# Re-listing the first steps of a linear-attention and feed-forward kernel in an order found by search

## The chip, the cores and the metric

The kernel runs on one core of one Trainium2 chip. The core has five engines with a queue of instructions each: PE (TensorE, the matmuls), DVE (VectorE), ACT (ScalarE), POOL (GpSimd) and SP (SyncE, which only starts transfers here). The time is the device time of one execution in microseconds (us). It is given as the median of several runs; a separate profiled execution gives the trace.

## The reference

Two layers follow each other. The first is a linear attention with a decaying state, for 4 batches, 8 heads, 768 tokens and a head dimension of 48:

```python
for t in range(S):
    cur = np.einsum('bhd,bhe->bhde', u[None] * kt, vt)
    y[:, :, t] = np.einsum('bhd,bhde->bhe', rt, state + cur)
    state = w[None, :, :, None] * state + np.einsum('bhd,bhe->bhde', kt, vt)
...
h = x @ w_in
g = np.maximum(0.01 * h, h)
return (g @ w_out)
```

The second takes y as x, 3072 tokens by 384, through w_in (384 by 2048), a leaky ReLU and w_out (2048 by 384). Inputs and outputs are float32.

## The kernel before

The 768 tokens of a batch are cut into 6 chunks of 128. One pair n of chunk and batch (24 in all, n = 4 x chunk + batch) is the unit of work. Within a chunk the recurrence becomes matmuls: r and k are scaled by tables of powers of w, turned so that the head dimension lies on partitions, multiplied to a 128 x 128 matrix per head (masked to the tokens that lie earlier, with the term of u on its diagonal), and this matrix times v plus turned r times the state gives y. The state of a batch goes from pair n to pair n + 4. y is copied to bfloat16 as a slice of xT, the input of the second layer, which runs on 128 tokens (pairs 0 to 3) or 256 tokens (from pair 4 on) at a time.

All work is a list of named steps, the string ORDER. `run` (it reads the names from left to right) calls one function for each, and each function appends instructions to the program. Two things follow from a step's place in the list. First, every engine plays its own instructions in the order in which they were appended; nothing passes on an engine. The class Sched finds the data each step reads and writes and adds semaphore waits between engines where one needs another's result. Second, the eight PSUM banks are handed out and given back in the order of the list (`take`, `give`), so a step that takes a bank waits until the step that gave it back has read it.

The names of the steps, with n the pair:

- `k0`, `r0`: loads of pair 0 in float32 (`load_first`, L234). `k0` is issued by ACT, `r0` by SP. `kn`, `rn`, `vn` for the other pairs: loads issued by POOL (`load_one`, L243). `wi0` to `wi3` and `wo0` to `wo3`: quarters of w_in and w_out, issued by POOL (L253, L257). `w8`, `w`, `u8`, `u`: small rows of w and u, issued by SP.
- `c0q@`, `c0k@`: casts of pair 0's r and k to bfloat16 on DVE (L440). `Cw`, `Wl`, `E`: w as columns on PE (L557), its logarithm wcol and the turned tables on ACT (L576, L356). `bc`, `lnw`, `qtab`, `ktab`: w spread to all partitions on PE (L337), its logarithm and the two tables on ACT (L344, L351). `Cu`, `C`: the columns of w times u on PE and their copy on DVE (L568, L583), after `wu8` (L361). `u16`, `U`, `utab`: the table of u.
- `one`, `ones`, `qk0`, `v0z`, `v0y`, `wlz`, `zr`: memsets on DVE. `trow`, `tcol`: indices on POOL (L275, L270). `tri`, `id`, `id8`, `exps`: mask, identities and exponents from them, on DVE. `table`: ACT's load of its function table. `F9`, `F6`, `F4`: that many matmuls of ones by ones into a bank, whose result nobody reads (L290).
- `Pnq`, `Pnk`: scaled r and k on DVE (L392). `Tnq`, `Tnk` and `tnq`, `tnk`: turning on PE (L455) and the copy out on ACT (L473, on DVE for pair 0 with its tables, L468). From pair 6 on `XnT`, a transposing transfer issued by SP, takes their place.
- `Xn`, `Dn`, `Qn` for n up to 3: the diagonal term, as a product on DVE (L407), matmuls on PE (L512) and scaled v on DVE (L414). From pair 4 on `qn` are the row sums on DVE (L421, L423, L425) and `Qn` the diagonal tile on POOL (L432).
- `An`, `Mna`, `Mnb`: the matrix on PE (L484) and its masking on DVE, in two halves (L493, from pair 4 L497). `Yn`, `yn`: y on PE (L646, L653) and its copy to xT on ACT (L667). `Kn`, `Sn`, `sn`: k by v on PE (L538, L529) and the new state on DVE. `W`: the decay table for the state on ACT (L591).
- `Gn.f`, `gn.f`: four blocks of x by w_in for one pair on PE (L692) and their leaky ReLU on ACT (L703). `Jm.f`, `jm.f`: two blocks for two pairs. `Hn`, `hn`: the product with w_out on PE (L716), its copy on ACT (L728) and the store by SP.

Around the change the order is thus the list itself. Two lines say which queue the first loads stand in:

```python
eng, queue = {"k": ("act", A), "r": ("sp", SP)}[which]
add(eng, lambda: queue.dma_start(dst, src), W=[(which, n)], dma=f"{which}{n}")
```

The functions that read the list:

Of the kernel before, what the change touches and what calls it, by code (L numbers as in the profile page):

```python
# [18 lines left out]
E = 64  # L19
# [6 lines left out]
TURNED, DIAG, CARRY, EXACT, RAW = 6, 4, 4, 1, 1  # L26
STRIPS = 8
ORDER = """
w8 qk0 k0 v0z one r0 trow ones v0y tcol wlz r1 id8 F9 wi1 u8 zr table Cw Wl id E w bc lnw c0q@ T0q c0k@ tri u exps k1
T0k u16 wu8 Cu t0q t0k qtab P1q F6 k3 v3 U A0 ktab T1q v0 t1q X0 C D0 P1k T1k t1k F4 M0b P3k M0a T3k K3 utab X1 A1 D1  # L30
Q0 Y0 t3k P0k r3 P3q M1a T3q r2 P2q y0 k2 K0 M1b v1 Q1 W G0.1 Y1 t3q X3 wi3 A3 y1 g0.1 S3 T2q D3 G1.1 g1.1 k5 t2q r5
r4 P2k T2k wi2 S0 v2 M3b t2k Q3 G0.3 g0.3 G1.3 k4 M3a Y3 P5k A2 y3 P4q T4q v4 wi0 T5k v5 wo3 t4q g1.3 G3.1 q5 t5k Q5
G3.3 g3.3 P5q r6 wo2 X2 g3.1 M2b D2 wo1 G3.2 Q2 G0.2 g0.2 T5q t5q K2 P4k T4k M2a t4k S2 G1.2 g3.2 q4 Q4 K1 S1 Y2 A5 A4
G1.0 y2 G2.1 M5a G0.0 G2.3 M4a M5b Y5 g0.0 y5 M4b Y4 y4 G2.2 g2.2 K4 J2.4 j2.4 k6 wo0 J2.1 J2.2 g1.0 g1.2 S4 k7 P6q q6
j2.1 P6k P7k G2.0 r7 q7 X6T J2.6 j2.6 J2.3 j2.3 k8 G3.0 J2.7 j2.7 k9 r9 j2.2 J2.5 P7q g3.0 g2.3 X7T J2.0 H1 h1 r8 q8
g2.0 Q6 P9k j2.0 P8k H0 j2.5 H3 Q7 A6 P9q X9T P8q X8T v6 A7 M6a v7 M7a g2.1 H2 h2 v9 v11 v10 M6b Y6 M7b y6 Q8 q9 Y7 y7
K5 r11 K6 S6 r10 k10 S5 Q9 v8 K7 S7 h0 h3 k11 J3.0 j3.0 J3.1 j3.1 J3.2 j3.2 J3.3 j3.3 J3.4 j3.4 J3.5 j3.5 J3.6 j3.6
J3.7 j3.7 A8 A9 M8a M8b M9a M9b P10q P10k X10T P11q P11k X11T k12 r12 v12 k13 r13 v13 q10 Q10 q11 Q11 H4 h4 Y8 Y9 y8
y9 K8 K9 S8 S9 s8 s9 H5 h5 J4.0 j4.0 J4.1 j4.1 J4.2 j4.2 J4.3 j4.3 J4.4 j4.4 J4.5 j4.5 J4.6 j4.6 J4.7 j4.7 P12q P12k
X12T P13q P13k X13T q12 q13 A10 A11 M10a M10b M11a M11b k14 r14 v14 k15 r15 v15 Q12 Q13 H6 h6 H7 h7 Y10 Y11 y10 y11  # L40
K10 K11 A12 A13 M12a M12b M13a M13b S10 S11 P14q P14k X14T P15q P15k X15T s10 s11 q14 q15 J5.0 j5.0 J5.1 j5.1 k16 r16
v16 k17 r17 v17 Q14 Q15 J5.2 j5.2 J5.3 j5.3 J5.4 j5.4 J5.5 j5.5 J5.6 j5.6 J5.7 j5.7 H8 h8 H9 h9 Y12 Y13 y12 y13 K12
K13 A14 A15 M14a M14b M15a M15b S12 S13 P16q P16k X16T P17q P17k X17T s12 s13 q16 q17 J6.0 j6.0 J6.1 j6.1 k18 r18 v18
# [3 lines left out]
K17 A18 A19 M18a M18b M19a M19b S16 S17 P20q P20k X20T P21q P21k X21T s16 s17 q20 q21 J8.0 j8.0 J8.1 j8.1 k22 r22 v22  # L47
k23 r23 v23 Q20 Q21 J8.2 j8.2 J8.3 j8.3 J8.4 j8.4 J8.5 j8.5 J8.6 j8.6 J8.7 j8.7 H14 h14 H15 h15 Y18 Y19 y18 y19 K18
K19 A20 A21 M20a M20b M21a M21b S18 S19 P22q P22k X22T P23q P23k X23T s18 s19 q22 q23 J9.0 j9.0 J9.1 j9.1 Q22 Q23 J9.2
j9.2 J9.3 j9.3 J9.4 j9.4 J9.5 j9.5 J9.6 j9.6 J9.7 j9.7 H16 h16 H17 h17 Y20 Y21 y20 y21 A22 A23 M22a M22b M23a M23b  # L50
J10.0 j10.0 J10.1 j10.1 J10.2 j10.2 J10.3 j10.3 J10.4 j10.4 J10.5 j10.5 J10.6 j10.6 J10.7 j10.7 H18 h18 Y22 Y23 y22
y23 H19 h19 J11.0 j11.0 J11.1 j11.1 J11.2 j11.2 J11.3 j11.3 J11.4 j11.4 J11.5 j11.5 J11.6 j11.6 J11.7 j11.7 H20 h20
H21 h21 H22 h22
# [784 lines left out]
```

## Time and profile before

| what | value |
|---|---|
| median of 3 runs | 168.88 us (168.47 to 169.81) |
| profiled execution, its time | 167.93 us |
| profiled execution, its span (first to last instruction) | 166.1 us |
| busy share of PE, DVE, ACT, POOL | 96%, 65%, 54%, 66% |

The profile comes from one execution. Its page gives busy times by engine, the chain of work that ended last, and groups of instructions by line. Its timeline lists instructions in order of time: start, duration, engine, line, operation, output <- inputs, shapes, how many of a kind follow each other and, in brackets, how long the engine stood idle before and what ended that. "L392" is line 392 of the kernel. "PEld" is PE's loading of weights, "SPq", "ACTq" and "POOLq" an issue of a transfer on that engine's queue. A matmul's end is modelled, so a duration holds the way through the array too; the pitch from one start to the next is closer to what it costs.

### The profile page before, as it was taken

What the parts mean: (1) busy time and instruction counts of PE and PEld (TensorE: products, weight loads), DVE (VectorE), ACT (ScalarE), POOL (GpSimd) and SP (SyncE); (2) the same over time, 40 slices, a digit from 0 to 9 for tenths busy, and PEclk for the clock granted to TensorE, in tenths of its full rate; (3) what the DMA queues carried; (4) which work ended last, traced back from release to release, by engine and by line L of the source; (5) the groups of instructions that cost most, each with busy time, mean ns of one, the idle gap of its engine ahead of it and who ended that gap; (6) DMA issues with size and microseconds to landing.
All of it is one profiled execution on the core that took longest, in us unless ns stands there. A gap on an engine that the chain in (4) does not pass through costs nothing.

```text
span 166.1 us, 5157 instructions
## 1 busy us (share of the span) xinstructions
PE 158.9 (96%) x2220; PEld 120.6 (73%) x2220; DVE 107.8 (65%) x248; ACT 89.3 (54%) x168; POOL 110.4 (66%) x125
## 2 busy tenths in 40 slices
PE   2798999999999999999999999999999999999994
PEld 2576989985567668668768768768678668678663
DVE  7799998377688599958938939939939934000000
ACT  3856873865138438436536546447437438449121
POOL 8999798987999949999299299399380270000000
PEclk9999999999999999999999999999999999999999
DMA  7999999999999995999949949969960540011012
GB/s 107 145 141 162 170 188 193 178 150 165 99 153 233 119 167 128 125 159 151 146 105 116 145 112 110 113 160 103 137 148 14 99 126 4 0 47 51 37 57 97
DMA packets 101268, 20.19 MB, mean 122 GB/s; under 512 B 94459, under 2 KB 101246, under 8 KB 101246
## 3 DMA queue, kind: packets, MB, share of 16 engines
q0 software_dynamic: 76512, 10.03, 93.2%
q1 hardware_dynamic: 23694, 9.65, 27.9%
q8 instruction: 17, 0.28, 0.7%
q10 hardware_dynamic: 1040, 0.20, 0.6%
q14 instruction: 5, 0.04, 0.1%
HBM read 20.45 MB, written 4.72 MB: 152 GB/s over the span
## 4 chain that ended last, share of the span: by engine, by line
PE 85%; POOL 7%; DMA 4%; DVE 2%; issue 0%; ACT 0%; POOLq 0%
PE ps L716 38%; PE ps L692 36%; PE ps L653 6%; DMA r_sb<-in_r_dram 4%; PE ps L484 3%; POOL r_sb L243 2%; POOL k_sb L243 2%; POOL v_sb L243 2%; PE ps L529 1%; POOL w_in_sb L253 1%; DVE prod L407 1%; PE ps L538 1%; DVE s_tok L425 0%; PE ps L455 0%; POOL trow L275 0%
## 5 line engine op out<-in xcount | busy, mean ns | idle before, releaser
L692 PE MATMUL ps<-xT,w_in_sb 128*128 128x256 bf16 (+1 forms) x672 | 66.4, 257 | 0.2
L703 ACT ACTIVATE gT<-ps 128x512 bf16<-128x512 f32 x96 | 56.3, 598 | 16.1 <-PE ps L692 12.3
L716 PE MATMUL ps<-w_out_sb,gT 128*128 128x384 bf16 (+2 forms) x400 | 64.6, 320 | 0.0
L692 PEld LDWEIGHTS ps<-xT,w_in_sb 128*128 128x128 bf16 x672 | 57.0, 98 | 7.2 <-DVE sum_t L614 0.5
L432 POOL TENSOR_TENSOR at<-ident,s_tok 128x512 bf16<-128x512 bf16 x40 | 42.1, 1087 | 24.9 <-DVE s_tok L425 24.9
L716 PEld LDWEIGHTS ps<-w_out_sb,gT 128*128 128x128 bf16 x400 | 38.1, 98 | 23.1
L728 ACT ACTIVATE out_sb<-ps 128x384 f32<-128x384 f32 (+2 forms) x25 | 11.9, 479 | 51.1 <-PE ps L716 51.1
L497 DVE CAST_PREDICATED at<-mask,ps 128x512 bf16<-128x512 uint16 x40 | 24.9, 685 | 20.1 <-PE ps L484 19.9
L243 POOL DMA_DIRECT2D v_sb<-in_v_dram x24 | 22.1, 928 | 0.0
L243 POOL DMA_DIRECT2D k_sb<-in_k_dram x23 | 21.2, 927 | 0.0
L243 POOL DMA_DIRECT2D r_sb<-in_r_dram x23 | 21.1, 926 | 0.1
L423 DVE TENSOR_TENSOR rku<-r_sb,ku 128x384 bf16<-128x384 bf16 x20 | 12.2, 612 | 1.4 <-DMA r_sb<-in_r_dram 0.8
L667 ACT ACTIVATE xT<-ps 128x384 bf16<-128x384 f32 x24 | 10.8, 491 | 2.5 <-PE ps L653 2.4
L425 DVE TENSOR_REDUCE s_tok<-rku 128x8 f32<-128x384 bf16 x20 | 11.1, 553 | 0.7
L392 DVE TENSOR_TENSOR qk<-k_sb,ktab 128x384 bf16<-128x384 bf16 x23 | 10.0, 437 | 1.3 <-DMA k_sb<-in_k_dram 1.3
L653 PE MATMUL ps<-at,v_sb 128*32 128x128 bf16 x384 | 10.6, 219 | 0.0
L653 PEld LDWEIGHTS ps<-tp,st 128*32 128x32 bf16 x240 | 7.3, 96 | 3.0 <-issue 2.5
L392 DVE TENSOR_TENSOR qk<-r_sb,qtab 128x384 bf16<-128x384 bf16 x23 | 8.9, 390 | 0.4 <-DMA r_sb<-in_r_dram 0.2
L653 PE MATMUL ps<-tp,st 128*32 128x128 bf16 x240 | 9.1, 221 | 0.0
L653 PEld LDWEIGHTS ps<-at,v_sb 128*32 128x32 bf16 x384 | 8.6, 97 | 0.4
L605 DVE TENSOR_TENSOR sum_t<-ps,st 64x192 bf16<-64x192 f32 x24 | 8.5, 353 | 0.6
L421 DVE TENSOR_TENSOR ku<-k_sb,u_tab 128x384 bf16<-128x384 bf16 x20 | 7.9, 395 | 1.2 <-DMA k_sb<-in_k_dram 1.1
(67 smaller groups left out, 96.0 us busy)
## 6 DMA issues: line engine op xcount, KB each, us to landing
out_dram<-out_sb SPq DMA_DIRECT2D x23, 192.0 KB, 2.0
v_sb<-in_v_dram POOLq DMA_DIRECT2D x24, 96.0 KB, 4.5
r_sb<-in_r_dram POOLq DMA_DIRECT2D x23, 96.0 KB, 4.9
k_sb<-in_k_dram POOLq DMA_DIRECT2D x23, 96.0 KB, 4.7
w_in_sb<-in_moe_w_in_dram POOLq DMA_DIRECT2D x4, 384.0 KB, 6.6
w_out_sb<-in_moe_w_out_dram POOLq DMA_DIRECT2D x4, 384.0 KB, 7.2
tp<-qk SPq DMA_TRANSPOSE x18, 4.7
k_f<-in_k_dram ACTq DMA_DIRECT2D x1, 192.0 KB, 2.8
```

The costliest lines, as they stand in the source:

```text
L243: add("pool", lambda: G.dma_start(dst, src), R=pace, W=[(which, n)], dma=f"{which}{n}")
L392: add("dve", lambda: V.tensor_tensor(qk[iq][:, H * half:H * half + H, 0:D], hd(src), hd(tab[:, :]), ALU.mult), R=[(name, n), "qk"[half] + ...
L423: add("dve", lambda: V.tensor_tensor(rku[i2][:, :], r_of(n), ku[i2][:, :], ALU.mult), R=[("r", n), ("ku", i2)], W=[("rku", i2)])
L425: add("dve", lambda: V.tensor_reduce(s_tok[i2][:, :], hd(rku[i2][:, :]), AX.X, ALU.add), R=[("rku", i2)], W=[("s", i2)])
L432: add("pool", lambda hh=hh, s_of=s_of: G.tensor_tensor(at[ia][:, hh, :, :], ident[:, :].unsqueeze(1).to_broadcast([128, NP, 128]), s_of.un ...
L497: add("dve", lambda: V.copy_predicated(at[n % NAT][:, hh, :, :], mask[:, :].bitcast(mybir.dt.uint16).unsqueeze(1).to_broadcast([128, NP, 1 ...
L653: last = PE.matmul(ps_y[32 * q:32 * q + 32, 128 * s:128 * s + 128], a, m, start=not whole and step == 0, stop=step == len(columns[q]) - 1)
L667: add("act", lambda: A.activation(xT[ix][:, :, 128 * slot:128 * slot + 128], ps_y[:, 0:HD].rearrange("p (s t) -> p s t", t=128), AF.Copy), ...
L692: last = PE.matmul(ps_g[:, step * f:step * f + step], w_in_sb[:, s, 128 * fb:128 * fb + 128], xT[ix][:, s, t], start=s == 0, stop=s == NSL ...
L703: add("act", lambda: A.activation(gT[ig][:, fb0:fb0 + count, t], ps_g[:, :].rearrange("p (f t) -> p f t", t=128 * width), AF.Prelu, alpha= ...
L716: last = PE.matmul(ps_o[:, 0:c1 - c0], gT[ig][:, s, 128 * slot:128 * slot + 128], w_out_sb[:, s, c0:c1], start=s == 0, stop=s == NFB - 1)
L728: add("act", lambda: A.activation(out_sb[io][:, c0:c1], ps_o[:, 0:c1 - c0], AF.Copy), R=[key], W=held)
```

## The change

The string ORDER is replaced by another order of the same steps. The steps of pairs 0 to 3, and with them loads, tables, memsets and most of what pairs 4 to 13 need up to the paired products J3, are listed as a search found them, which used a model of the program with the durations of a trace. Near the end `H17 h17` moves behind `M23b`. No function is changed. The core of the diff:

```diff
@@ ORDER, first part @@
-w8 qk0 k0 v0z one r0 trow ones v0y tcol wlz r1 id8 F9 wi1 u8 zr table Cw Wl id E w bc lnw c0q@ T0q c0k@ tri u exps k1
-T0k u16 wu8 Cu t0q t0k qtab P1q F6 k3 v3 U A0 ktab T1q v0 t1q X0 C D0 P1k T1k t1k F4 M0b P3k M0a T3k K3 utab X1 A1 D1
-Q0 Y0 t3k P0k r3 P3q M1a T3q r2 P2q y0 k2 K0 M1b v1 Q1 W G0.1 Y1 t3q X3 wi3 A3 y1 g0.1 S3 T2q D3 G1.1 g1.1 k5 t2q r5
-r4 P2k T2k wi2 S0 v2 M3b t2k Q3 G0.3 g0.3 G1.3 k4 M3a Y3 P5k A2 y3 P4q T4q v4 wi0 T5k v5 wo3 t4q g1.3 G3.1 q5 t5k Q5
-G3.3 g3.3 P5q r6 wo2 X2 g3.1 M2b D2 wo1 G3.2 Q2 G0.2 g0.2 T5q t5q K2 P4k T4k M2a t4k S2 G1.2 g3.2 q4 Q4 K1 S1 Y2 A5 A4
-G1.0 y2 G2.1 M5a G0.0 G2.3 M4a M5b Y5 g0.0 y5 M4b Y4 y4 G2.2 g2.2 K4 J2.4 j2.4 k6 wo0 J2.1 J2.2 g1.0 g1.2 S4 k7 P6q q6
-j2.1 P6k P7k G2.0 r7 q7 X6T J2.6 j2.6 J2.3 j2.3 k8 G3.0 J2.7 j2.7 k9 r9 j2.2 J2.5 P7q g3.0 g2.3 X7T J2.0 H1 h1 r8 q8
-g2.0 Q6 P9k j2.0 P8k H0 j2.5 H3 Q7 A6 P9q X9T P8q X8T v6 A7 M6a v7 M7a g2.1 H2 h2 v9 v11 v10 M6b Y6 M7b y6 Q8 q9 Y7 y7
-K5 r11 K6 S6 r10 k10 S5 Q9 v8 K7 S7 h0 h3 k11 J3.0 j3.0 J3.1 j3.1 J3.2 j3.2 J3.3 j3.3 J3.4 j3.4 J3.5 j3.5 J3.6 j3.6
-J3.7 j3.7 A8 A9 M8a M8b M9a M9b P10q P10k X10T P11q P11k X11T k12 r12 v12 k13 r13 v13 q10 Q10 q11 Q11 H4 h4 Y8 Y9 y8
...
+v0z wlz one w8 ones F9 trow r0 v1 qk0 w tcol tri table zr F6 id id8 Cw v0 Wl E r1 bc lnw qtab exps u k1 k0 c0q@ v0y u8
+wu8 T0q c0k@ t0q@ r3 Cu C P1q ktab T0k t0k@ T1q A0 X0 u16 U P1k M0a T1k F4 D0 t1q k3 P3k T3k t1k A1 wi1 M0b Q0 v3 k2
+t3k X1 Y0 y0 P3q T3q M1a r2 D1 M1b K3 G0.1 t3q g0.1 Q1 Y1 y1 P2k utab A3 X3 D3 P2q M3b W T2q M3a t2q P0k T2k t2k wi3
+G1.1 Q3 G0.3 k5 P5k K0 S0 r4 P4q G1.3 r5 X2 g1.1 wi2 Y3 A2 g0.3 k4 y3 T4q T5k t5k v2 G3.3 g3.3 g1.3 wi0 P5q T5q M2b S3
+G3.1 v5 t4q G1.2 D2 wo1 G0.2 v4 q5 wo3 t5q G3.2 r6 P4k T4k M2a g3.1 g3.2 Q2 g0.2 A5 Y2 wo2 K1 Q5 G0.0 y2 G2.1 q4 t4k
+g0.0 S1 Q4 A4 G2.3 M5a M5b g2.3 G1.0 k6 M4a K2 Y5 M4b Y4 wo0 K4 S2 G2.2 y5 y4 J2.2 J2.6 J2.1 S4 k7 q6 g1.0 J2.5 P6q
+P6k X6T j2.2 r7 P7q g2.1 G3.0 j2.5 J2.4 j2.1 j2.4 P7k X7T v7 J2.0 q7 g3.0 k9 J2.3 G2.0 J2.7 H0 j2.6 P9k j2.0 r9 r8 P8q
+k8 H3 Q6 r10 g1.2 g2.2 j2.3 j2.7 g2.0 H1 A6 P8k k10 A7 v8 H2 q8 P9q M6b X8T v6 M6a Q7 M7a v12 Y6 Q8 X9T h1 P10q M7b Y7
+h3 K7 k12 K6 q9 y6 K5 S5 S7 y7 J3.0 j3.0 h0 P10k v10 q10 v9 r13 J3.5 J3.2 J3.7 S6 j3.5 J3.1 A8 j3.7 A9 k11 r12 P12k
+P13q j3.1 k13 r11 H4 J3.3 h2 Q9 J3.6 v13 M8b M8a J3.4 P12q K8 M9b X12T Y8 h4 X10T K9 Q10 j3.4 M9a j3.3 S8 s8 q11 j3.6
+P13k S9 Y9 P11k v11 j3.2 s9 X13T y8 P11q X11T y9 Q11 H5 h5 J4.0 j4.0 J4.1 j4.1 J4.2 j4.2 J4.3 j4.3 J4.4 j4.4 J4.5 j4.5
...
@@ ORDER, near the end @@
-j9.2 J9.3 j9.3 J9.4 j9.4 J9.5 j9.5 J9.6 j9.6 J9.7 j9.7 H16 h16 H17 h17 Y20 Y21 y20 y21 A22 A23 M22a M22b M23a M23b
+j9.2 J9.3 j9.3 J9.4 j9.4 J9.5 j9.5 J9.6 j9.6 J9.7 j9.7 H16 h16 Y20 Y21 y20 y21 A22 A23 M22a M22b M23a M23b H17 h17
```

On the engines this makes, among others, the following difference. ACT issues `k0` as its first instruction before and behind `qtab` after. SP issues w8, r0, u8, w, u before and w8, r0, w, u, u8 after. POOL issues r1, wi1, k1, k3, v3, v0, r3, r2, k2, v1, wi3 first before; after it is v1, v0, r1, k1, r3, k3, wi1, v3, k2, r2, wi3. DVE's queue begins with the memsets of qk before, and with those of v, wl, wu, one and ones after. On PE, F6 follows F9 directly after; before, it stood behind `T0k` and `Cu`.

More of the change, by code (lines that the diff above doesn't have):

```diff
@@ L39 @@
-y9 K8 K9 S8 S9 s8 s9 H5 h5 J4.0 j4.0 J4.1 j4.1 J4.2 j4.2 J4.3 j4.3 J4.4 j4.4 J4.5 j4.5 J4.6 j4.6 J4.7 j4.7 P12q P12k
-X12T P13q P13k X13T q12 q13 A10 A11 M10a M10b M11a M11b k14 r14 v14 k15 r15 v15 Q12 Q13 H6 h6 H7 h7 Y10 Y11 y10 y11
+v0z wlz one w8 ones F9 trow r0 v1 qk0 w tcol tri table zr F6 id id8 Cw v0 Wl E r1 bc lnw qtab exps u k1 k0 c0q@ v0y u8
+wu8 T0q c0k@ t0q@ r3 Cu C P1q ktab T0k t0k@ T1q A0 X0 u16 U P1k M0a T1k F4 D0 t1q k3 P3k T3k t1k A1 wi1 M0b Q0 v3 k2
+t3k X1 Y0 y0 P3q T3q M1a r2 D1 M1b K3 G0.1 t3q g0.1 Q1 Y1 y1 P2k utab A3 X3 D3 P2q M3b W T2q M3a t2q P0k T2k t2k wi3
@@ L41 @@
+h3 K7 k12 K6 q9 y6 K5 S5 S7 y7 J3.0 j3.0 h0 P10k v10 q10 v9 r13 J3.5 J3.2 J3.7 S6 j3.5 J3.1 A8 j3.7 A9 k11 r12 P12k
+P13q j3.1 k13 r11 H4 J3.3 h2 Q9 J3.6 v13 M8b M8a J3.4 P12q K8 M9b X12T Y8 h4 X10T K9 Q10 j3.4 M9a j3.3 S8 s8 q11 j3.6
+P13k S9 Y9 P11k v11 j3.2 s9 X13T y8 P11q X11T y9 Q11 H5 h5 J4.0 j4.0 J4.1 j4.1 J4.2 j4.2 J4.3 j4.3 J4.4 j4.4 J4.5 j4.5
+J4.6 j4.6 J4.7 j4.7 q12 q13 A10 A11 M10a M10b M11a M11b k14 r14 v14 k15 r15 v15 Q12 Q13 H6 h6 H7 h7 Y10 Y11 y10 y11
 K10 K11 A12 A13 M12a M12b M13a M13b S10 S11 P14q P14k X14T P15q P15k X15T s10 s11 q14 q15 J5.0 j5.0 J5.1 j5.1 k16 r16
```

## The prediction

> **What bounds the kernel now.** I read the page first, then the chain of work that ended last in order of time, the waits, busy time by stretches, and then the timelines of the single engines for the first 31 us, since the edits lie there.
>
> ```profile
> span 166.1 us, 5157 instructions
> PE 158.9 (96%) x2220; PEld 120.6 (73%) x2220; DVE 107.8 (65%) x248; ACT 89.3 (54%) x168; POOL 110.4 (66%) x125
> ```
>
> ```profile
> 12.76 5.88 DMA r_sb<-in_r_dram
> ...
> 20.54 1.19 DVE prod L407
> ...
> 30.54 6.58 PE ps L692 x72
> ...
> 136.42 0.04 issue
> ```
>
> ```profile
> 13.72:30.54 16.82, 16.01 (x359) 14.51 (x360) 14.37 (x30) 11.41 (x24) 15.26 (x18) 1.00 1.77 181
> 30.54:163.80 133.26, 133.15 (x1756) 99.00 (x1754) 82.28 (x182) 69.88 (x130) 82.14 (x87) 1.00 1.13 114
> ```
>
> ```profile
> PE ps L646 <- DVE vs L414: 0.4, 1, 0.4
> ...
> PE ps L512 <- DVE prod L407: 0.4, 1, 0.4
> ```
>
> Over the span PE is 96% busy. In the windows (length, then busy of PE, PEld, DVE, ACT, POOL) it is 133.15 of 133.26 us from 30.54 on, so there an order can win only a tenth of a microsecond. From 13.72, where the first w_in product (G0.1) starts, to 30.54, where the paired products (J2) start, PE is idle for 16.82 - 16.01 = 0.81 us: two waits for DVE, 0.4 before Y1 and 0.4 before the diagonal of pair 2. The rest is the start. Whatever moves G0.1 moves the end by nearly as much, because from there PE works off a list of fixed length. DVE feeds PE up to G0.1, so its queue comes next; the first column gives each step's pitch (start to next start).
>
> ```profile
> 5.12 0.34 DVE L440 CAST raw<-k_f 128x384 bf16<-128x384 f32 x1
> 5.38 0.58 DVE L300 TENSOR_SCALAR mask<-trow,tcol 128x128 bf16<-128x128 f32 x1
> ...
> 7.08 1.29 DVE L468 TENSOR_TENSOR tp<-ps,turned 128x512 bf16<-128x512 f32 x2 [1.11 <-PE ps L455]
> 8.28 0.35 DVE L392 TENSOR_TENSOR qk<-r_sb,qtab 128x384 bf16<-128x384 bf16 x1
> 8.55 0.42 DVE L407 TENSOR_TENSOR prod<-tp 128x512 bf16<-128x512 bf16 x1
> 8.88 0.35 DVE L583 CAST wu<-ps 48x4 bf16<-48x4 f32 x2
> 9.53 0.36 DVE L392 TENSOR_TENSOR qk<-k_sb,ktab 128x384 bf16<-128x384 bf16 x1 [0.29 <-DMA k_sb<-in_k_dram]
> 9.92 0.69 DVE L493 TENSOR_TENSOR at<-ps,mask 128x512 bf16<-128x512 f32 x1
> 10.52 0.35 DVE L392 TENSOR_TENSOR qk<-k_sb,ktab 128x384 bf16<-128x384 bf16 x1
> ...
> 11.72 0.55 DVE L414 TENSOR_TENSOR vs<-v_sb,ps 128x384 bf16<-128x384 bf16 x1
> 12.19 0.55 DVE L392 TENSOR_TENSOR qk<-k_f,ktab 128x384 bf16<-128x384 f32 x1
> ```
>
> **The change, part by part.** The edits reorder instructions; no work is added or removed. I take the parts in order of time.
>
> *1. The load of pair 0's k moves from the head of ACT's queue to behind qtab.* This part decides. `k0` is the one load that ACT issues, before as its first instruction. In the new list it stands behind `Cw Wl E bc lnw qtab`: ACT's queue holds the table load, wcol, the four turned tables, lnw and qtab, and only then the issue. lnw waits for PE's `bc`, and `bc` for the row w.
>
> ```profile
> 0.73 0.43 ACTq L234 DMA_DIRECT2D k_f<-in_k_dram  x1
> ...
> 2.18 0.61 SPq L735 DMA_DIRECT2D w_row<-in_w_dram  x1
> ...
> 5.42 1.01 PE L337 MATMUL ps<-w_row,one_row 1*128 1x192 f32 x4 [0.81 <-DMA w_row<-in_w_dram]
> ...
> 6.47 0.49 ACT L344 ACTIVATE lnw<-ps 128x384 f32<-128x384 f32 x1
> ...
> 7.27 0.60 ACT L351 ACTIVATE qtab<-lnw,tcol 128x384 bf16<-128x384 f32 x1
> ```
>
> That an issue stands behind waiting compute of its engine shows on POOL, where a load comes only after a pair of diagonal tiles that itself waited for DVE:
>
> ```profile
> 20.36 2.27 POOL L432 TENSOR_TENSOR at<-ident,s_tok 128x512 bf16<-128x512 bf16 x2 [0.88 <-DVE s_tok L425]
> ...
> 22.57 0.95 POOL L243 DMA_DIRECT2D r_sb<-in_r_dram  x1
> ```
>
> w was SP's fourth issue, at 2.18, and released PE at 5.42, 3.24 us later. It becomes the third, about 0.5 us earlier, so bc starts at 4.91 and ends 1.01 later at 5.92, and lnw (0.49) ends near 6.45. `k0` is then issued between 6.45 (qtab is only handed over) and 7.05 (qtab's 0.60 is done too); I take 6.6, near the first. Its time to landing:
>
> ```profile
> w_in_sb<-in_moe_w_in_dram POOLq DMA_DIRECT2D x2, 384.0 KB, 6.1
> ...
> k_sb<-in_k_dram POOLq DMA_DIRECT2D x4, 96.0 KB, 6.0
> ...
> k_f<-in_k_dram ACTq DMA_DIRECT2D x1, 192.0 KB, 2.8
> r_f<-in_r_dram SPq DMA_DIRECT2D x1, 192.0 KB, 3.1
> ```
>
> The lower end is k_f's own 2.8, when little else was in flight; the upper end is the 6.0 of POOL's loads in the flow. I take 3.3, nearest r_f (same size, same kind of issue, 3.1 beside k_f), with a little more for POOL's flow. So k lands at 9.9, with bounds of 9.25 and 13.0, and the cast of k starts at 9.95, not at 5.12: **4.83 us later**. A page of the Trainium skill, DMA: Bandwidth & Descriptors, section "Issuing engines are not separate DMA queues", says that loads from all issuing engines run on the same 16 DMA engines and interleave; by it the late load would not get the 2.8 of the early one, and no row of this trace has such a load in the midst of POOL's.
>
> *2. What waits behind that cast on DVE.* The new DVE queue has the cast of k ahead of all that feeds PE: t0q, C, P1q, t0k, D0, P1k, M0a, P3k, M0b, Q0. None can pass it, though most of their inputs are there earlier. Only the gaps of v (v0y) and wu8 stand in its shadow. From 9.95, by pitches of the rows above: cast 0.26, t0q 0.60 (half of 7.08 to 8.28), C 0.35, P1q 0.27, t0k 0.60, D0 0.33, P1k 0.39, M0a 0.60, P3k 0.27, M0b 0.60 (as M0a), Q0 0.47. The sum is 4.74, so Q0 ends at 14.69. Before, it ended at 12.19, 7.07 after that cast began, with 1.11 of waiting for the turns, 0.29 for k1, and the mask, D1 and others in between. So 2.33 of the 4.83 come back, and **Q0 is 2.50 us late**. The earlier first memsets, the fills in one piece, mask and wu8 ahead of time: I cost all of them at nothing, since they end in the shadow of the same wait.
>
> *3. PE up to G0.1.*
>
> ```profile
> 8.77 0.61 PE L484 MATMUL ps<-tp 48*128 48x128 bf16 x8
> ...
> 10.34 0.63 PE L290 MATMUL ps<-ones 128*128 128x128 bf16 x4
> 10.93 0.61 PE L455 MATMUL ps<-ident,qk 128*128 128x128 bf16 x4
> ...
> 12.46 0.33 PE L646 MATMUL ps<-ident,vs 128*128 128x128 bf16 x3
> ...
> 13.07 0.40 PE L455 MATMUL ps<-ident,qk 128*128 128x128 bf16 x4
> 13.30 0.33 PE L538 MATMUL ps<-v_sb,qk 128*128 128x96 bf16 x4
> 13.72 0.84 PE L692 MATMUL ps<-xT,w_in_sb 128*128 128x128 bf16 x12
> ```
>
> The same four turning matmuls take 0.61 us at 10.93 and 0.40 at 13.07: PE runs at a slower rate until about 12.3. In the new order it has little to do between the turn of r (about 6.4) and the turn of k (10.3), so it is dense only from A0, at 12.1, and I keep the slow rate up to G0.1. T1k follows P1k (12.8): T1k 0.4, F4 0.45, D0 0.25, T3k 0.4, A1 0.6, to 14.9. Then Y0 (0.61 from 12.46 to 13.07, estimated at 0.9 slow) to 15.8, T3q 0.4, D1 and K3 together 0.5: **G0.1 at 16.7, 2.98 us late**. y0, one copy out of PSUM like lnw (0.49), is done by 16.4. w_in's first part is now POOL's seventh load; six at 0.95 from about 1.3 on put its issue at 7.0, and 6.1 more land it at 13.1. Its cover is the late k: were G0.1 ready before 13.1, this would be next.
>
> *4. G0.1 to J2.* Both orders hold the same 14 products G and the same turns, A, K and Y here, but K0 (about 0.2) now stands behind G0.1: PE's 16.01 become 16.2. The idle 0.81 goes: on the new DVE queue Q1 is done at about 17.1, before G0.1 is, and D2 near 21.8, some 2.5 ahead of its matmuls, since POOL's Q5, beside which it stalled for part of its 1.19, now comes after it. J2 starts at 16.7 + 16.2 = 32.9, not 30.54: **+2.36**. Two corrections cancel as far as I can tell: some 0.5 of short waits that PE's modelled ends count as busy, and as much for matmuls slow to about 17.7 (1.0 at half rate).
>
> *5. Loads, POOL and the rest.* The 5.88 us of r_sb in the old chain go, without gain: DVE asks for that load at 23 instead of 18.6. Q5 and Q4 follow their row sums (24.2 and 27.0, by the same pitches) and end at 26.3 and 29.1; M4b ends near 30.3, and G2.2, which takes its bank, is due at 31.9: covered by 1.6. SP's transposes follow k6 to k9, which POOL issues about 2 us later, as late as PE itself. From J2 on PE's list keeps its length; H17 behind M23b takes away at most the 0.04 of issue at 136.42. All this at 0.
>
> **Sum.** +2.98 (G0.1) + 0.19 (K0) - 0.81 (idle) = +2.36, rounded to 2.3. The profiled execution took 167.93 us, 1.83 more than its span; with 2.3 more it is 170.2. The median of the runs is 168.88, 0.95 above it, so I forecast 168.88 + 2.3 = **171.2 us**.
>
> **Rivals.**
>
> *A, within 1%.* k lands at its lower bound, 0.65 earlier, and 0.7 of hidden waits and slow matmuls go too: 2.3 - 1.35 = +0.95, 169.8. For it: the landings of 2.8 and 3.1. Against it: the 6.0 of the loads in the flow.
>
> *B, slower still.* PE stays slow. It was dense from about 6.4 and changed at 12.3, 5.9 us on; 12.1 + 5.9 is 18.0, and one such change missed could make it 19.2, 1.5 beyond my 17.7, 0.75 at half rate. With k landing 1.2 later, at 11.1, that is 2.3 + 0.75 + 1.2 = +4.25, 173.1. A page of the Trainium skill, TensorE: Matmul & The Clock Gate, Part 1, says that PE's clock is halved until a free-running window of about 3.4 us has been busy; by it the change could come anywhere from 15.5 to 18.9. The trace agrees with a jump after dense work, though it took 5.9.
>
> *C, faster.* The issue of `k0` is not held by ACT's waiting compute. Then DVE passes the cast at about 6.4, behind wu8, Q0 ends 4.74 later at 11.1, 1.05 early, and with 0.81 of idle gone and K0's 0.19 the time is 168.88 - 1.67 = 167.2. It decides from a landing before 7.5: there the 2.36 are used up. Against it stands POOL's load at 22.57.
>
> **How the numbers follow.** About 1% (1.7 us) is what a measurement of this kernel can tell from no change. The forecast has a chance of 0.50, A 0.27, B 0.16, C 0.07. So slower by over 1% has 0.66, within 1% 0.27, faster 0.07. The range from 169.4 to 173.4 leaves out C, the lower part of A and the tail of B: under 2 in 10.
>
> **What would show it.** Right: ACT's issue of k_f at 6.4 to 7.1; DVE's cast of k at 9.3 to 11, with a wait for that load ahead of it; Q0's end near 14.7; G0.1 near 16.7; J2 near 32.9; no idle PE of note between them. Wrong: the issue of k_f near 1 us, or a cast before 7.5 (C); G0.1 at 16.7 but J2 well before 32.4, so that the hidden waits are larger than I hold; a PE gap after J2 at a diagonal tile or a load of pairs 6 to 13, which I cost at nothing.

## The result, and the profile after

The changed kernel took 178.05 us (median of 6 runs, 176.77 to 178.72) against 168.37 for the kernel before beside it (6 runs, 168.09 to 169.81). The ratio is 1.0558, with a 95% interval of 1.0505 to 1.0611: slower by 5.6%, above the forecast range of 169.4 to 173.4. Here and below a ratio leaves disturbed runs out, so it can differ from the quotient of two medians. The profiled execution took 177.91 us.

The page of the kernel after, its span and its busy times:

```profile
span 176.1 us, 5154 instructions
PE 161.2 (92%) x2220; PEld 122.0 (69%) x2220; DVE 108.1 (61%) x248; ACT 88.8 (50%) x168; POOL 110.2 (63%) x125
```

PE was 96% busy and is 92% busy now. Its busy time grew by 2.3 us (158.9 to 161.2) and its idle time by 7.7, so most of the 10.0 us in the span is waiting. Where it came in is seen by cutting both spans at the same steps of PE: the starts of the first w_in product (G0.1), of the first paired product (J2), of J4 and of J5. The columns are the stretch, its length, and busy time (count) of PE, PEld, DVE, ACT, POOL, then the granted clock, the busy share of the DMA engines and the GB/s that they moved. First the kernel before, then the kernel after:

```profile
13.72:30.37 16.65, 15.84 (x357) 14.35 (x358) 14.37 (x30) 11.27 (x23) 15.09 (x18) 1.00 1.76 181
30.37:62.33 31.96, 31.93 (x408) 22.95 (x406) 24.38 (x46) 16.62 (x32) 28.30 (x31) 1.00 1.89 157
62.33:75.39 13.06, 13.06 (x203) 9.69 (x200) 10.28 (x24) 7.10 (x13) 13.06 (x15) 1.00 1.42 149
```

```profile
19.01:36.17 17.16, 17.16 (x365) 15.48 (x363) 14.61 (x31) 12.53 (x26) 9.70 (x12) 1.00 1.34 144
36.17:69.93 33.76, 32.42 (x408) 23.17 (x406) 25.64 (x53) 15.05 (x31) 28.87 (x32) 1.00 2.00 149
69.93:84.64 14.71, 13.07 (x202) 9.68 (x200) 8.34 (x17) 7.10 (x13) 14.71 (x16) 1.00 1.29 123
```

The clock reads 1.00 in all six rows, also where PE's pitch shows half that rate (below), so at the start of these two kernels the rate is read from the pitch. The rows have these answers. Up to G0.1: 19.01 against 13.72, **+5.29**. G0.1 to J2: 17.16 against 16.65, +0.51; there PE is busy throughout, so the two old waits went, as forecast, but busy time rose by 1.32. J2 to J4: 33.76 against 31.96, **+1.80**, of which 1.34 is idle (33.76 - 32.42). J4 to J5: 14.71 against 13.06, **+1.65**, idle 1.64. The rest of the 10.0 (5.29 + 0.51 + 1.80 + 1.65 = 9.25) came late: J10.0 starts at 146.46 instead of 136.47, 9.99 later.

The start first, from the timeline of the kernel after (start, duration, engine, line, operation; in brackets the idle time before and its releaser):

```profile
3.89 1.01 PE L337 MATMUL ps<-w_row,one_row 1*128 1x192 f32 x4
4.21 1.70 ACT L356 ACTIVATE turned<-trow,wcol 128x256 bf16<-128x256 f32 x4
5.82 0.47 ACT L344 ACTIVATE lnw<-ps 128x384 f32<-128x384 f32 x1
6.32 0.61 ACT L351 ACTIVATE qtab<-lnw,tcol 128x384 bf16<-128x384 f32 x1
6.33 0.42 ACTq L234 DMA_DIRECT2D k_f<-in_k_dram  x1
...
11.29 0.87 DVE L440 CAST raw<-k_f 128x384 bf16<-128x384 f32 x1 [5.38 <-DMA k_f<-in_k_dram]
...
12.22 0.61 PE L455 MATMUL ps<-ident,raw 128*128 128x128 bf16 x4 [5.93 <-DVE raw L440]
...
14.19 0.61 PE L484 MATMUL ps<-tp 48*128 48x128 bf16 x8
...
16.32 0.55 DVE L414 TENSOR_TENSOR vs<-v_sb,ps 128x384 bf16<-128x384 bf16 x1
16.79 0.42 DVE L407 TENSOR_TENSOR prod<-tp 128x512 bf16<-128x512 bf16 x1
...
18.18 0.61 PE L455 MATMUL ps<-ident,qk 128*128 128x128 bf16 x4
...
19.01 1.48 PE L692 MATMUL ps<-xT,w_in_sb 128*128 128x128 bf16 x12
...
21.88 0.61 PE L455 MATMUL ps<-ident,qk 128*128 128x128 bf16 x8
```

k's load is issued at 6.33, as soon as qtab is handed over, and DVE waits 5.38 us for it with its whole list behind; PE waits 5.93 for DVE. Q0 ends at 16.79. The whole delay is there at A0 already, which starts at 14.19 against 8.77 before (+5.42); from A0 to G0.1 PE takes 4.82 us against 4.95. The rows at 18.18 and 21.88 show PE's rate: 0.61 us for four turning matmuls, then the same time for eight.

Behind J2, the chain of work that ended last passes through four transfers that the chain of the kernel before doesn't pass:

```profile
36.02 6.79 DMA r_sb<-in_r_dram
...
43.88 7.46 DMA tp<-qk
...
72.70 4.47 DMA tp<-qk
...
139.44 3.95 DMA tp<-qk
```

The first is the load of r7, which X7T needs. Each of the last three, the transposes X7T, X11T and X23T, is followed in the chain by the second step of a diagonal pair on PE (A7 at 51.48, A11 at 77.30, A23 at 143.52). A diagonal pair is here the steps An and An+1 of two neighbouring pairs; before, the second of these four followed the first by 0.23 or 0.24 us. A fourth wait, before A9, is not for a transfer. PE's waits from 42 to 84 us, where the kernel before has none:

```profile
PE ps L484 <- DMA tp<-qk: 2.1, 2, 1.6
PE ps L484 <- ACT out_sb L728: 0.9, 1, 0.9
```

The timeline around A9:

```profile
59.56 0.40 PE L484 MATMUL ps<-tp 48*128 48x128 bf16 x8
...
59.76 2.11 POOL L432 TENSOR_TENSOR at<-ident,s_tok 128x512 bf16<-128x512 bf16 x2
60.16 0.48 ACT L728 ACTIVATE out_sb<-ps 128x384 f32<-128x384 f32 x1
60.16 0.55 DVE L614 TENSOR_TENSOR sum_t<-ps,st 128x384 bf16<-128x384 f32 x1
60.75 1.84 DVE L616 TENSOR_TENSOR st<-sum_t,wl 128x384 bf16<-128x384 bf16 x1
...
60.81 0.40 PE L484 MATMUL ps<-tp 48*128 48x128 bf16 x8 [0.86 <-ACT out_sb L728]
```

A8 starts at 59.56 and A9 at 60.81; before, the two stood 0.23 apart. The profile names ACT's copy, done at 60.64. By the program's order of PSUM banks, A9 takes the banks that S6 (DVE's sum_t, done at 60.71) and j3.5 (a leaky ReLU on ACT ahead of that copy) give back, and S6 stands behind P10k and q10 in the new DVE list. ACT's copy and S6 end within 0.07 us of each other; two experiments below bear on which it is.

### The profile page after: what moved, and what is told of

Its sections match the earlier page's. It is cut to its first block, busy times and chain, and to the rows that moved or that the text cites. A ratio compares the mean times of both kernels' runs of the same rounds, so it can differ in the third digit from the quotient of the medians.

```text
span 176.1 us, 5154 instructions
## 1 busy us (share of the span) xinstructions
PE 161.2 (92%) x2220; PEld 122.0 (69%) x2220; DVE 108.1 (61%) x248; ACT 88.8 (50%) x168; POOL 110.2 (63%) x125
## 4 chain that ended last, share of the span: by engine, by line
PE 62%; DMA 16%; DVE 13%; POOL 4%; issue 2%; ACT 2%; POOLq 0%; DVEq 0%
PE ps L716 28%; PE ps L692 22%; DMA tp<-qk 9%; PE ps L653 5%; DMA r_sb<-in_r_dram 4%; PE ps L484 3%; DMA k_f<-in_k_dram 3%; DVE qk L392 3%; DVE sum_t L605 2%; DVE at L493 1%; DVE st L623 1%; DVE at L497 1%; POOL at L432 1%; DVE ku L421 1%; POOL k_sb L243 1%
## 5 line engine op out<-in xcount | busy, mean ns | idle before, releaser
L703 ACT ACTIVATE gT<-ps 128x512 bf16<-128x512 f32 x96 | 55.6, 601 | 16.4 <-PE ps L692 12.7
L692 PEld LDWEIGHTS ps<-xT,w_in_sb 128*128 128x128 bf16 x672 | 57.9, 99 | 6.6 <-DVE sum_t L614 0.2
L392 DVE TENSOR_TENSOR qk<-r_sb,qtab 128x384 bf16<-128x384 bf16 x23 | 10.2, 444 | 5.1 <-DMA r_sb<-in_r_dram 4.9
L484 PE MATMUL ps<-tp 48*128 48x128 bf16 x192 | 9.2, 227 | 3.7 <-DMA tp<-qk 2.5
L423 DVE TENSOR_TENSOR rku<-r_sb,ku 128x384 bf16<-128x384 bf16 x20 | 11.5, 575 | 0.7
L653 PE MATMUL ps<-at,v_sb 128*32 128x128 bf16 x384 | 11.2, 227 | 0.0
L484 PEld LDWEIGHTS ps<-tp 48*128 48x128 bf16 x192 | 5.9, 98 | 6.3 <-issue 2.5
L473 ACT ACTIVATE tp<-ps 128x512 bf16<-128x512 f32 x10 | 5.8, 599 | 8.2 <-PE ps L455 8.1
L392 DVE TENSOR_TENSOR qk<-k_sb,ktab 128x384 bf16<-128x384 bf16 x23 | 8.9, 389 | 1.0 <-DMA k_sb<-in_k_dram 1.0
```

The source lines that it names most:

```text
L392: add("dve", lambda: V.tensor_tensor(qk[iq][:, H * half:H * half + H, 0:D], hd(src), hd(tab[:, :]), ALU.mult), R=[(name, n), "qk"[half] + ...
L423: add("dve", lambda: V.tensor_tensor(rku[i2][:, :], r_of(n), ku[i2][:, :], ALU.mult), R=[("r", n), ("ku", i2)], W=[("rku", i2)])
L484: last = PE.matmul(at_bank[n][hh][0][:, 128 * p:128 * p + 128], tp[it][rows, NP + p, :], tp[it][rows, p, :], start=True, stop=True)
L653: last = PE.matmul(ps_y[32 * q:32 * q + 32, 128 * s:128 * s + 128], a, m, start=not whole and step == 0, stop=step == len(columns[q]) - 1)
L692: last = PE.matmul(ps_g[:, step * f:step * f + step], w_in_sb[:, s, 128 * fb:128 * fb + 128], xT[ix][:, s, t], start=s == 0, stop=s == NSL ...
L703: add("act", lambda: A.activation(gT[ig][:, fb0:fb0 + count, t], ps_g[:, :].rearrange("p (f t) -> p f t", t=128 * width), AF.Prelu, alpha= ...
```

## The experiments

**Two theories.** Mine, after the result: two separate causes, the late load of pair 0's k (the start) and a few places behind J2 where the new order leaves a diagonal pair without cover (A7, A9, A11, A23: 0.6 + 1.0 + 1.8 + 0.6 us). The rival: one cause, the late start, and the later waits are only its echo, because loads and DVE fall behind with it. A second rival for the start: not the late k itself, but PE's slow rate, prolonged by PE's idle time.

**k's load back at the head.** In the changed kernel one step is moved:

```diff
-tri table zr
+tri k0 table zr
...
-exps u k1 k0 c0q@
+exps u k1 c0q@
```

> The changed kernel with one step moved: k0 (pair 0's k) is again ACT's first issue. Theory 1 (two separate costs: the late k load at the start, and four places further down where the new order itself makes PE wait): G0.1 starts near 13.7 instead of 19.0, so about 5 us come back, and the four waits of PE (0.6 before A7, 1.0 before A9, 1.8 before A11, 0.6 before A23) stay: about 173 us. Theory 2 (one cause: the late k load, and the later waits only follow from POOL's and the transfers' delay): all ten come back, 168 us. A third outcome, G0.1 still near 17 or later, would put the start's loss on other moved steps (POOL's loads, the fills).

Measured: 172.98 us (4 runs), ratio 1.0266 (1.0221 to 1.0312). k is issued at 0.74, G0.1 is at 14.16, J2 at 30.93: the start's 5 us are back. The four diagonal pairs are still apart, 0.88 (A6 to A7), 0.88, 2.15 and 0.82 us, against 0.84, 1.26, 2.04 and 0.83 in the kernel after and 0.23 or 0.24 before. So the later waits are no echo. S6's sum ends at 55.04 here and A9 starts at 55.14, the same 0.10 us later as in the kernel after (60.71 and 60.81), while the profile now names another operation of ACT.

**The kernel before, with k's load late.** The opposite edit in the kernel before, with the load moved from the head to behind lnw and qtab; qtab moves forward with it:

```diff
-w8 qk0 k0 v0z one
+w8 qk0 v0z one
...
-bc lnw c0q@ T0q
+bc lnw qtab k0 c0q@ T0q
...
-t0q t0k qtab P1q
+t0q t0k P1q
```

> The kernel before with two steps moved: qtab and k0 stand right behind lnw, so that pair 0's k is issued as late as in the changed kernel; all else is the old order. Theory 1: G0.1 moves from 13.7 to 18.5 or 19, and the end by 4.5 to 5.5 us (173 to 174), with no PE wait of note after J2. Theory 2: the same start, but then waits of PE at A7, A9 or A11 like those of the changed kernel, 176 or more. If the price of the late load is only what my prediction gave it, 171.

Measured: 174.86 us (4 runs), ratio 1.0385 (1.0326 to 1.0444), 0.9 above the range of the first theory, with none of the four waits (A12 and A13 stand 0.80 apart, 0.38 before). In the answer for the tile k_f, the operations and the time from issue to landing:

```profile
L234 ACTq DMA_DIRECT2D k_f<-in_k_dram x1: 424/424/424, 7.0 to 7.0; - x1
L440 DVE CAST raw<-k_f x1: 364/364/364, 12.6 to 12.6; 128x384 bf16<-128x384 f32 x1
...
DMA to landing us min/median/max: 5.6/5.6/5.6
```

One late load alone makes the old order 3.85% slower. It took 5.6 us to land, against 2.8 from the head of the queue and 4.9 in the kernel after. G0.1 was at 20.16, 1.2 later than expected; k was issued at 6.98 and landed at 12.60, 1.33 later than in the kernel after.

**The load half as late.** In the changed kernel k0 stands between Wl and E, behind one ACT instruction that waits for PE, ahead of all tables:

```diff
-Cw v0 Wl E r1
+Cw v0 Wl k0 E r1
...
-exps u k1 k0 c0q@
+exps u k1 c0q@
```

> The changed kernel with one step moved: k0 stands between Wl and E, so that its load is issued at about 4.2 us, behind one ACT instruction that waits for PE (until 4.0) and ahead of the six table steps. My theory: the landing takes what the loads issued beside it take then (3.8 to 4.0 against 4.9 at 6.33), k is there at 8.1 instead of 11.3, PE's pair 0 starts 3.1 us sooner, and G0.1 follows one to one until the front's other chains bind (they bind from a landing of about 6.1 on): G0.1 at 15.9 to 16.5, time 174.5 to 175.5, the four late waits unchanged. Rival: what costs the start is not when k lands but where its cast stands in DVE's list; then G0.1 stays at 18 to 19 and the time at 176.5 to 178.

Measured: 175.07 us (4 runs), ratio 1.0374 (1.0336 to 1.0411); G0.1 at 16.50. The time is as expected, but not the landing:

```profile
L234 ACTq DMA_DIRECT2D k_f<-in_k_dram x1: 426/426/426, 4.0 to 4.0; - x1
L440 DVE CAST raw<-k_f x1: 731/731/731, 8.9 to 8.9; 128x384 bf16<-128x384 f32 x1
...
DMA to landing us min/median/max: 4.9/4.9/4.9
```

It took 4.9 us, not 3.8 to 4.0, and POOL's r_sb, issued at 3.44, landed at 8.68 where it had landed at 7.10 in the kernel after. The two loads were under way together, and r_sb took 5.23 us instead of 3.66. From here to the kernel after, k lands 2.37 later (8.90 to 11.27), G0.1 is 2.51 later and the kernel takes 2.98 more: near one to one, as expected. The four late waits are still there (0.59, 1.26, 2.14 and 1.35 us apart).

**The cast last.** What of the start is due to the list behind the cast on DVE? In the changed kernel everything that doesn't need k goes ahead of the cast:

```diff
-T0q c0k@ t0q@ r3 Cu C P1q ktab T0k t0k@ T1q A0 X0 u16 U P1k M0a T1k F4 D0 t1q k3 P3k T3k t1k A1
+T0q t0q@ Cu C P1q ktab P1k T1q t1q T1k t1k c0k@ r3 T0k t0k@ A0 X0 u16 U M0a F4 D0 k3 P3k T3k A1
```

> The changed kernel with the late k load, but the cast of k no longer ahead of the rest on DVE: t0q, C, P1q and P1k, with Cu, ktab and the turns of pair 1, stand before it. This tells the blocked queue from pair 0's own chain. If the 4.9 us that DVE stands still are the loss, about 1.6 us of its work (t0q 0.6, C 0.35, P1q 0.3, P1k 0.35) come back: G0.1 at 17.4, 176.4. If pair 0's chain (cast, turn, A0, mask, Q0, Y0) sets it alone, G0.1 stays within 0.5 us of 19.0 and the time with it.

Measured: 176.18 us (4 runs), ratio 1.0454 (1.0406 to 1.0503). G0.1 is at 17.27, 1.74 earlier than after. But k landed 0.66 earlier too (10.61), by the spread of a load in the flow, which leaves about 1.1 us for DVE's list. The kernel with the four places put back (below) has the changed order up to J2; there k landed at 11.10 and G0.1 came at 18.34. Against it the gain is 1.07 with a landing 0.49 earlier, which leaves 0.6. So 0.6 to 1.1 of the 5.29 is DVE's list, and the larger part is the late landing and pair 0's own chain behind it.

**PE kept busy in the wait.** Fill matmuls (they multiply ones, their result is not used) in the gap of PE, to bring the faster rate forward; first 50 behind Cu, then, in another run, 75 there and 8 ahead of T1q:

```diff
-r3 Cu C P1q
+r3 Cu F50 C P1q
```

```diff
-r3 Cu C P1q ktab T0k t0k@ T1q
+r3 Cu F75 C P1q ktab T0k t0k@ F8 T1q
```

> The changed kernel with 50 more matmuls of ones (F50) behind Cu, in the time in which PE waits for the late k load; their result is read by nobody. If the slow rate of PE (0.61 instead of 0.40 for four turning matmuls, until about 21.5) is what made the start 2.3 us worse than forecast, PE is fast from the turn of k on and G0.1 starts at about 17.5, the end 1.0 to 2 us earlier (176 to 177). If DVE alone sets the start, G0.1 moves by under 0.5 us and the time by no more.

> The changed kernel with the late k load, and with 75 matmuls of ones behind Cu and 8 ahead of T1q, so that PE is busy from the turn of r to the turn of k and on; the 50 of the run before made it fast at 10.1, but it had nothing to do from then to 11.6 and was slow again from 13.5 to 20.3. If the slow rate costs what the two counts of time say (PE's matmuls from A0 to about 21.4 at half rate), G0.1 comes at 17.4 to 18 and the time is 1.2 to 2 us under the changed kernel's: 176 to 176.8. If DVE is the limit there, G0.1 stays at 18.3 to 19.

Measured: 176.52 us (ratio 1.0398, 1.0294 to 1.0503) and 176.84 (1.0475, 1.042 to 1.053), 4 runs each. Neither tested what it was made for, since the fast rate came and went again before G0.1. The windows of the kernel with 50 fills (length, PE's busy time, then PEld, DVE, ACT, POOL, and behind them the granted clock):

```profile
6.70:10.10 3.40, 3.40 (x35) 3.40 (x33) 0.00 (x0) 1.16 (x3) 3.40 (x5) 1.00 1.84 133
10.10:13.50 3.40, 1.71 (x24) 1.19 (x21) 2.24 (x6) 0.23 (x1) 3.40 (x5) 1.00 1.74 170
13.50:16.90 3.40, 3.34 (x36) 2.33 (x36) 3.37 (x9) 1.56 (x3) 3.40 (x5) 0.50 1.89 181
16.90:20.30 3.40, 3.40 (x55) 2.91 (x56) 2.57 (x6) 1.49 (x3) 3.40 (x6) 0.50 1.98 172
20.30:23.70 3.40, 3.40 (x78) 3.16 (x70) 2.72 (x6) 3.18 (x9) 1.66 (x3) 0.99 1.85 179
```

The clock reads 1.00 in the first row too, where the fills follow each other every 0.107 us; from 10.1 on the pitch is 0.056. PE is dense to 10.1, runs at the fast rate from there, is busy for 1.71 of the next 3.40 us, and then the granted clock is 0.50 for two stretches; G0.1 came at 18.38, again at the slow rate. With 75 fills it was 18.49, with the clock at half from 17.1 to 20.5. So the share of the slow rate in the start is not settled by these two. A hint lies in the spread: the four executions with 50 fills took 173.72, 176.32, 176.73 and 177.41 us, with a mean granted clock of 1.00 in the first and 0.98 in the others. No trace of the first was kept, so it stays a hint that the rate costs some us here.

**The four places put back.** In the changed kernel: H17 and h17 back ahead of Y20 (for A23), S6 ahead of P10k (A9), P11k P11q X11T ahead of S8 (A11), Q6 ahead of v7 (A7):

```diff
-j2.1 j2.4 P7k X7T v7 J2.0
+j2.1 j2.4 P7k X7T Q6 v7 J2.0
...
-h0 P10k v10
+h0 S6 P10k v10
...
-j3.3 S8 s8
+j3.3 P11k P11q X11T S8 s8
...
-H16 h16 Y20
+H16 h16 H17 h17 Y20
```

> The changed kernel with the late k load left as it is and the four later places undone: H17 and h17 ahead of Y20 again; S6 ahead of P10k and q10 on DVE; P11k, P11q and X11T ahead of S8; Q6 ahead of the loads v7, k9, r9, r8, k8 on POOL, so that these no longer stand beside the transposing transfer X7T. Theory 1: each of the four waits goes by itself, G0.1 and J2 stay at 19.0 and 36.2, and the time is about 4 us less (174). Theory 2 (they follow from the late start): only H17's 0.6 goes, 177.

Measured: 175.56 us (4 runs), ratio 1.0422 (1.0353 to 1.049). That is between the two theories. All four diagonal pairs stand 0.23 us apart, as the first has it, but only 2.5 us of the span came back (176.1 to 173.6), and 0.74 of that lies ahead of J2 (35.43 instead of 36.17), where nothing was changed. Other waits opened between A7 and J4. In the list of PE's waits from 40 to 72 us:

```profile
PE ps L653 <- DVE at L497: 1.6, 2, 1.1
PE ps L692 <- DVE at L497: 0.7, 1, 0.7
```

PE now waits there for DVE's masked copies, and DVE for r_sb (5.2 us in that stretch). The two edits together, k's load first and the last three of the four places:

> The changed kernel with k0 as ACT's first issue and three of the later places undone: H17 and h17 ahead of Y20, S6 ahead of P10k and q10, and P11k, P11q, X11T ahead of S8. POOL's order is left alone. Theory 1 (each wait belongs to one place): against the version with k0 alone (172.98) the waits before A9 (0.65), A11 (1.9) and A23 (0.6) go and that before A7 (0.65) stays: about 169.8. If undoing a place only hands the wait to the next step in DVE's queue, as it did for Y6 and J3.6 when Q6 was moved, 171 or more.

Measured: 170.64 us (4 runs), ratio 1.0131 (1.0114 to 1.0148). It is 0.8 above what was expected and 0.4 below the rival's 171. A9's wait is gone in both kernels that move S6, which with the 0.10 us above speaks for S6 as its cause. A7's wait is gone here without moving Q6, as in the two kernels with fills and the one with the cast last: X7T took 5.3 us here, 6.7, 6.4 and 6.5 there, 7.46 in the kernel after and 3.05 before. It is a race between a transfer and PE, which the new order made close: X7T takes 5.3 to 7.5 us in all eight kernels with the new order behind J2, and 3.05 to 3.9 in all five with the old one there (three of these follow below). What remains lies between Y6 and J4, 16.13 us here with 14.59 of PE busy, against 14.23 before. DVE is busy for 15.34 of these 16.13 us and was for 11.21 of the 14.23: the new list has P12 and P13 ahead of J4, the old one behind it.

**The new front with the old rest.** The changed order up to J2 with k0 first, behind it the old order:

> The changed order up to J2, with k0 as ACT's first issue, and from J2 on the old order. Theory 1: the new front with k0 early is worth the old one (G0.1 at 14.2 and J2 16.8 later, against 13.7 and 16.65), so the time is within 1 us of the kernel before, 168.5 to 169, and no PE wait of note follows J2. If the waits after J2 come from what the new front leaves behind (POOL's and DVE's backlog), they are here too: 171 or more.

Measured: 169.09 us (10 runs), ratio 1.0035 (1.0018 to 1.0052), within 1 us of the kernel before as expected, though J2 came 17.29 us after G0.1 and not 16.8. So the loss splits, by ratios times 168.4: 0.6 us for the new front with k first, 4.5 - 0.6 = 3.9 for the new order behind J2, and 9.4 - 4.5 = 4.9 for the place of one load.

**More fill in that front.** Can the front win once k is first? The last kernel with two more fills:

```diff
-wu8 T0q c0k@
+wu8 F5 T0q c0k@
...
-ktab T0k t0k@
+ktab T0k F8 t0k@
```

> The changed order up to J2 with k0 at the head, the order before behind it (the kernel of 169.09 us, ratio 1.0035), with 5 fill matmuls more ahead of T0q and 8 more behind T0k; they compute nothing that is used. What is left of that kernel's loss is by my theory the PE clock: its matmuls keep the slow pitch to about 15.5 to 17 us instead of 12.4, as PE has gaps of 0.5 to 0.9 us behind bc, T0q and T0k. If the gaps cause it, the fills bring the faster pitch forward by one to one and a half windows of 3.4 us, G0.1 takes 0.6 instead of 1.3 us, and the time is 168.2 to 168.6, level with the kernel before. Rival: the fills only delay T1q by 0.4 us and the pitch turns as late; then 169.2 to 169.6.

Measured: 169.60 us (12 runs), ratio 1.0054 (1.0026 to 1.0083). The faster rate came and the gain did not, so neither expectation held. PE's pitch is fast from 8.9 on instead of about 17.3, and G0.1 takes 0.67 instead of 1.27 us, but it starts at 13.96 instead of 14.16 and J2 at 31.73 instead of 31.45, since PE now waits:

```profile
PE ps L692 <- ACT tp L473: 1.1, 1, 1.1
PE ps L538 <- DMA v_sb<-in_v_dram: 1.0, 1, 1.0
```

(its waits from 13 to 32 us). So the slower pitch had covered these two chains. My theory that the PE clock is what is left of the loss falls. None of these kernels beats the one before.

**H17 alone.** The kernel before with H17 and h17 behind M23b:

```diff
-H16 h16 H17 h17 Y20 Y21 y20 y21 A22 A23 M22a M22b M23a M23b J10.0
+H16 h16 Y20 Y21 y20 y21 A22 A23 M22a M22b M23a M23b H17 h17 J10.0
```

> The kernel before with one of the late moves alone: the down-projection H17 and its h17 stand behind M23b instead of ahead of Y20. My theory: A22 and A23 come 2.6 us sooner on PE than X23T's landing allows, so PE waits about 0.6 us ahead of A23, and H17, which covered that wait, cannot; nothing behind it gives the time back, so the span grows by 0.4 to 0.6 us and the ratio is about 1.003. Rival (my forecast on record): H17 is filler anywhere, at most 0.04 us; ratio 1.000.

Measured: 169.45 us (12 runs), ratio 1.0059 (1.0034 to 1.0084). PE's waits from 120 us on, of which the kernel before has none:

```profile
PE ps L484 <- DMA tp<-qk: 0.8, 1, 0.8
```

A22 and A23 are 1.21 us apart, not 0.24, so the wait is longer than the 0.6 that was expected. This one move costs 0.6%, twice the expected 0.3%: H17, 2.6 us of matmuls, had covered the transpose X23T, and behind M23b it covers nothing.

## Why the prediction was wrong

*The direction and the deciding part were right.* Slower by over 1% had the largest chance, for the late k0. The issue (6.33, forecast 6.6), a wait of DVE for k ahead of the cast, and PE idle-free from G0.1 to J2 came as forecast. The time of the issue was in part luck: w released PE's bc at 3.89, not at 4.91, and lnw began only at 5.82, behind ACT's own four turned tables (from 4.21 on), not as soon as bc was done. DVE's wait was 5.38 us long, where the forecast's own times (6.4 to 9.95) give 3.55. C is ruled out: ACT issued the load only behind its waiting compute.

*Part 1, the landing, was mis-sized.* I took 3.3, near r_f's 3.1, since both are 192 KB loads by such an engine. It took 4.94. The rows to take were those of the loads around it in time: beside it r_sb, issued at 5.17, landed after 4.51, and k_sb, issued at 6.04, after 5.55, and in the trace of the kernel before POOL's loads issued at 5.93 and 6.79 landed after 5.55 and 5.50. The sentence of the Trainium skill that I cited (DMA: Bandwidth & Descriptors, "Issuing engines are not separate DMA queues") says that loads from all issuing engines run on the same 16 DMA engines and interleave. I had concluded from it that the late load would not get its early price; the runs agree, with 2.8 at the head and 4.3 to 5.6 in the flow. The bounds of 9.25 and 13.0 held the landing at 11.27.

*Parts 2 and 3, from the cast to G0.1, came out 2.31 late in all.* The cast began 1.34 late (11.29 for 9.95). From it to Q0's end took 5.50, not 4.74 (the step that the prediction calls D0 on DVE is X0); 0.53 of these 0.76 are the cast's own pitch, 0.79 for 0.26. The cast takes 0.33 to 0.87 us in these kernels, and what sets that stays open. From Q0 to G0.1 took 2.22, not 2.01.

*Part 4 had the wait right and the rate wrong.* The idle 0.81 went, but PE kept the slow rate to about 21.6, not 17.7, and not 19.2 as in rival B. PE was busy for 17.16 us where I had 16.2. J2 came at 36.17, not 32.9: 2.31 by G0.1 and 0.96 here. It is 1.13 here if J2 is counted from its first start in both kernels: before, that is 30.37, and my 30.54 came from the chain. The pitches account for it: G0.1, Y1 and A3 took 2.75 us (19.01 to 21.77), and at the faster pitch they take 0.67 (in the kernel with more fill), 0.62 and 0.32 (in the kernel before), 1.14 less. That is rival B's mechanism, and the start of +5.8 (36.17 - 30.37) is beyond B's +4.25. No run had this start at the fast rate throughout.

*Part 5 is the step that failed outright, a term put at nothing.* It reads: "From J2 on PE's list keeps its length; H17 behind M23b takes away at most the 0.04". The list kept its length; what went is the cover of four diagonal pairs. Their second steps came 0.61, 1.03, 1.81 and 0.60 us later behind the first than before, 4.05 us in all; by the kernel with k first the order behind J2 costs 3.9. I had checked POOL and the banks of pairs 4 and 5, and costed pairs 6 to 13 by the sentence that SP's transposes come as late as PE itself. Three of them came later than that or lost their cover. X7T was issued 5.4 us later, no later than PE, but took 7.46 instead of 3.05, with five of POOL's loads still under way at its issue where there had been one; that these loads lengthened it is argued, not isolated. X11T was issued 2.8 us ahead of the time at which A11 was due (72.70 to 75.50) instead of 7.7 (60.16 to 67.90), behind S9 and s9 on DVE. X23T lost the cover of H17, which alone cost 0.6% against my 0.04 us. A9 waited for the bank of S6, not for a transfer. The prediction did name "a PE gap after J2 at a diagonal tile" as what would make it wrong.

With the start at +5.80 instead of +2.36 and the four waits at 4.05 instead of nothing, the sum is 9.85 of the span's 10.0. Either of the two alone carries the forecast past its upper bound of 173.4: 168.88 + 5.80 = 174.7, and 171.2 + 4.05 = 175.3.

## What to carry to other kernels

When an order is changed, take each transfer that a step waits for and compare the work between its issue and its use, before and after, by durations; a step moved out of that stretch is a cost even where it is as long as ever elsewhere. Price a moved load by the loads that are under way beside it at its new place, not by its own old row, and look at which engine's waiting compute stands ahead of its issue. Where PE is at a slow rate, that rate may be covering other chains, so making it faster first shows what they cost.

## What the runs showed of the hardware

A load of 192 KB issued by ACT took 2.7 to 2.9 us as the first issue (six kernels), and 4.3 to 5.6 among POOL's loads (seven kernels). In the kernel with the load half as late, POOL's r_sb beside it landed 1.6 us later than without it.

PE's granted clock fell back to 0.50 after a stretch of 3.4 us in which PE was still busy for 1.71 (50 fills), and after one in which it was busy for 2.53 (75 fills, 13.69 to 17.11). The Trainium skill (TensorE: Matmul & The Clock Gate, Part 1) ties the slow clock to a window of idle; in these two runs a half and a quarter of such a window were enough.

DVE's products of bf16 in SBUF lengthen beside POOL's diagonal tiles: the one at 60.75 above took 1.84 us while POOL's pair ran from 59.76 to 61.87, and the same operation took 0.36, 0.61 and 0.89 at its three other times, with no such tile beside it. DVE's sum at 60.16, with one operand in PSUM, kept its 0.55 beside the same pair. That POOL is the cause is only argued here.
